# A second Strassen level for one more product of the last down projection: M7 split in seven, M6 ahead of it, operand sums of M7 and M4 on VectorE

## The chip, the cores and the metric

One core of one Trainium2 chip runs the whole kernel in one launch. The metric is the device time of one execution in microseconds (us), as the median of several runs. Engine names: PE is TensorE, DVE is VectorE, ACT is ScalarE, POOL is GpSimd, SP is SyncE, which here only issues DMAs.

## The reference

The input x has 2048 tokens of 1024 features, in bfloat16. The kernel is a layernorm, a linear-attention block and a gated feed-forward block, joined at the end:

```python
xn = _layernorm(x)
s = linear_attention(xn, wqkv, wo)            # 32 heads of 32
f = (silu(xn @ w_gate) * (xn @ w_up)) @ w_down  # 1024 -> 3584 -> 1024
out = x + s * silu(f)
```

What the change touches is the last matrix product, `h @ w_down`, with h of 2048 x 3584 and w_down of 3584 x 1024, for the second half of its tokens to be computed, and the two steps that follow it, silu and `x + s * g`.

## The kernel before

The feed-forward block runs in two passes of 1024 tokens. In each pass a loop of 28 steps (14 blocks of 256 columns of F, gate and up in turn) fills h, one 8-KB-per-partition weight tile a step; then comes the down projection. All products use Strassen's scheme in the form of Winograd: a product of 2x2 blocks is made from seven block products M1 to M7, whose operands are sums of blocks, and the results are added up afterwards.

The last pass's down projection is `emit_down_m`. h is seen as four blocks A11, A12, A21, A22, each of 512 tokens by 14 chunks of 128 of F. The sums S1 to S4 are made from them in place (S1 over A21, S2 over A11, S4 over A12), S3 in two tiles of its own (S3h). The weights of M1 to M7, sums of blocks of w_down, were made in the first pass and lie in DRAM. One product at the first level is 4 blocks of 128 tokens x 14 chunks = 56 matmuls of 512 columns; `prod_t(M, t, ...)` issues the 14 of one token block (L1439 in the profile).

M1, M2 and M4 (the tuple `L2`) go one level deeper: `l2_M` makes each from seven products again, each of 7 chunks x 2 token halves, with 256 columns (`l2_p`, L1475). Their operand sums are made by `l2_lhs`, four instructions for each of seven j, on POOL: for M2 all through the last pass into spare buffers (`x_spare`, "kept" in the profile), for M1 late in the pass into `r_spare`, for M4 during M7 into M2's buffers. `l2_M` moves part results between PSUM banks with copies on ACT (L1487, L1495) and adds to what is kept on DVE (L1427). It is a generator: it yields once after two products, and it calls `fill` between its sixth and its last product, so that another product's matmuls stand there on PE.

The second-level weights are prepared in the last pass's loop, in units of two j. `l2_load` (at the steps in `L2_UNITS`) has SP load four blocks into one of the two buffers in `r_spare`, which it takes in turn; `l2_sums`, one step later, makes four sums on POOL (L1149) and stores seven blocks to DRAM by a POOL DMA (L1150). The two buffers come out of the same eight as the weight tiles; from step `L2_FROM` on, POOL uses them for M1's operand sums. SP's queue is in program order: a load that waits for a buffer holds back the gate and up weights behind it.

The order on each engine is written by hand: it is the order of the program. In `emit_down_m` it is M1 and the first half of M2, M2 with M7's first token block as its fill, M7, M6, M5, M4 with M3's first token block as its fill, M3. KA holds M1 + ..., KB = KA + M7 + M6; `fin` multiplies by s and adds x (L1209, L1210) and has SP store the result, `flush` issues the waiting ones, and silu runs on ACT (L1461). `load(M, q)` lets SP go on to the weight tiles that follow in `w_seq`, in the order of `M_ORDER`, as buffers come free.

Of the kernel before, what the change touches and what calls it, by code (L numbers as in the profile page):

```python
# [10 lines left out]
ALU = mybir.AluOpType  # L11
# [10 lines left out]
def kernel(  # L22
# [11 lines left out]
    nc = tc.nc  # L34
# [13 lines left out]
    TPB = TB // P  # L48
# [4 lines left out]
    NFG = F // FW  # L53
# [133 lines left out]
    NPASS = NB // 2  # L187
    passes = list(range(NPASS - 1, -1, -1))
    NWA = NFG // 2
    M_ORDER = (1, 2, 7, 6, 5, 4, 3)  # L190
    L2 = (1, 2, 4)
    L2_ORDER = (1, 2, 5, 6, 7, 4, 3)
    L2_FROM = 20
    L2_UNITS = range(3, 18, 2)
    NQ = NFG // 2
    CH = CW // 2
    l2_drams = {}
# [756 lines left out]
    with ExitStack() as p3:  # L954
# [197 lines left out]
        def l2_bufs(M):  # L1152
            v = [x[:].rearrange("p a b -> p (a b)").bitcast(F16) for x in x_spare]
            if M == 1:
                v = [x[:].rearrange("p h a b -> p (h a b)").bitcast(F16) for x in r_spare]
            v = [x[:, 0:2 * NQ * 2 * P].rearrange("p (s j r n) -> p s j r n", s=2, j=NQ, r=2) for x in v]
            return [v[0][:, 0], v[0][:, 1], v[1][:, 0], v[1][:, 1]]

        def l2_quad(A, j):
            v = A[:, :, j].rearrange("p k (r t n) -> p k r t n", r=2, t=2)  # L1160
            return v[:, 0, :, 0], v[:, 1, :, 0], v[:, 0, :, 1], v[:, 1, :, 1]

        def l2_lhs(M, A, j, eng):
            a11, a12, a21, a22 = l2_quad(A, j)
            s1, s2, s3, s4 = [v[:, j] for v in l2_bufs(M)]
            eng.tensor_tensor(out=s1, in0=a21, in1=a22, op=ALU.add)
            eng.tensor_tensor(out=s2, in0=s1, in1=a11, op=ALU.subtract)
            eng.tensor_tensor(out=s3, in0=a11, in1=a21, op=ALU.subtract)
            eng.tensor_tensor(out=s4, in0=a12, in1=s2, op=ALU.subtract)

        def quads(h, a, t):
            return h[:].rearrange("p (j k a) t -> p k j a t", k=2, a=2)[:, :, :, a, t * TB:(t + 1) * TB]
# [230 lines left out]
        def emit_down_m(p, h, base):  # L1403
# [8 lines left out]
            def load(M, q=None):  # L1412

                n_ = max(i for i, key in enumerate(seq) if key[2][0] == M and q in (None, key[2][1])) + 1
                load_w_to(base + n_ + (NPK - 2 if M == 1 and q != 3 else NPK))

            def S3(k):
                return s3_[k // NWA][:, k % NWA]

            def lhs_of(M):  # L1420
                if M == 7:
                    return S3
                v = {1: A11, 2: A12, 3: S4, 4: A22, 5: S1, 6: S2}[M]
                return lambda k: v[:, k]

            def tt(out, a, b_, op=ALU.add):
                nc.vector.tensor_tensor(out=out, in0=a, in1=b_, op=op)  # L1427

            def sums(out, a, b_, op):
                for k in range(0, NFG, 2):  # L1430
                    tt(out[:, k:k + 2], a[:, k:k + 2], b_[:, k:k + 2], op)

            def w_of(M, k):
# [8 lines left out]
            def prod_t(M, t, out, first):  # L1442
                for k in range(NFG):
                    mm(M, t, k, out, first)
# [5 lines left out]
            def banks(n=TPB):  # L1450
                turn[0] += 1
                pool, tg = (pps, "s") if turn[0] % 2 else (ppm, "m")
                return [pool.tile([P, CW], FP32, name="dm", tag=tg)[:] for _ in range(n)]

            def kept(nm):
                v = [m4.tile([P, 2, CW], FP32, name=nm, tag="m4") for _ in range(TPB // 2)]
                return [v[t // 2][:, t % 2] for t in range(TPB)]

            def silu(c, nm):
                g_ = k2([P, CW], BF16, nm)[:]  # L1460
                nc.scalar.activation(out=g_, in_=c, func=ACT.Silu, scale=rch)  # L1461
                return g_
# [15 lines left out]
            def l2_M(M, A, K, done, fill, in_place, dst=None):  # L1478


                bk = banks()
                lo, hi = slice(0, CH), slice(CH, CW)
                xw, zy = bk[0::2], bk[1::2]
                for r in range(2):
                    l2_p(M, 1, r, A, bk)
                for r in range(2):
                    nc.scalar.copy(out=zy[r][:, hi], in_=xw[r][:, lo])  # L1487
                for r in range(2):
                    l2_p(M, 2, r, A, bk)
                load(M, 0)  # L1490
                yield
                for r in range(2):
                    l2_p(M, 5, r, A, bk)
                    l2_p(M, 6, r, A, bk)
                    nc.scalar.copy(out=zy[r][:, lo], in_=zy[r][:, hi])  # L1495
                load(M, 1)
                for r in range(2):
                    l2_p(M, 7, r, A, bk)
                if K is None:
                    c = [dst[0:2], dst[2:4]]  # L1500
                else:
                    c = [[k2([P, CW], FP32, "l2c")[:] for _ in range(2)] for r in range(2)]
                for r in range(2):
                    c0, c1 = c[r]
                    if K is None:
                        nc.scalar.copy(out=c1[:, hi], in_=zy[r][:, lo])
                        nc.scalar.copy(out=c0[:, hi], in_=zy[r][:, hi])
                        nc.scalar.copy(out=c0[:, lo], in_=xw[r][:, lo])
                    else:
                        tt(c1[:, hi], zy[r][:, lo], K[2 * r + 1][:, hi])  # L1510
                        tt(K[2 * r][:, hi] if in_place else c0[:, hi], zy[r][:, hi], K[2 * r][:, hi])
                        if not in_place:
                            tt(c0[:, lo], xw[r][:, lo], K[2 * r][:, lo])
                    tt(c1[:, hi], xw[r][:, hi], c1[:, hi])
                fill()
                for r in range(2):
                    l2_p(M, 4, r, A, bk)
                load(M, 2)
                for r in range(2):
                    c0, c1 = c[r]  # L1520
                    if K is None:
                        nc.scalar.copy(out=c1[:, lo], in_=zy[r][:, lo])
                    else:
                        tt(c1[:, lo], zy[r][:, lo], K[2 * r + 1][:, lo])
                        done(2 * r + 1, c1)
                    l2_p(M, 3, r, A, bk)
                    if in_place:
                        tt(c0, xw[r], K[2 * r])
                    else:
                        tt(c0[:, hi], xw[r][:, hi], c0[:, hi])  # L1530
                    if done is not None:
                        done(2 * r, c0)
                load(M, 3)

            def go(g):
                for _ in g:
                    pass

            fins = deque()

            def flush(n=99):
                while fins and n:
                    fin(p, *fins.popleft(), *EV)
                    n -= 1

            load_w_to(base + NPK - 2)
            KA = kept("kA")
            fins = deque()
            M7, M6, M5 = [], [], []
            KB = []  # L1550

            def fill7():
                M7.extend(banks())
                KB.extend(kept("kB"))
                prod_t(7, 0, M7[0], True)

            def done2(t, c):
                fins.append((t, 0, silu(c, "g11")))
            m2 = l2_M(2, quads(h, 1, 0), KA, done2, fill7, False)
            for k in range(NFG):  # L1560
                tt(S3(k), A11[:, k], A21[:, k], ALU.subtract)
            go(l2_M(1, quads(h, 0, 0), None, None, lambda: next(m2), False, KA))
            sums(S1, A21, A22, ALU.add)
            go(m2)
            sums(S2, S1, A11, ALU.subtract)
            for t in range(TPB):
                if t:
                    prod_t(7, t, M7[t], True)
                tt(KB[t], M7[t], KA[t])
                flush(1)  # L1570
            load(7)
            sums(S4, A12, S2, ALU.subtract)
            for j in range(NQ):
                l2_lhs(4, quads(h, 1, 1), j, nc.gpsimd)
            M6 = banks()
            for t in range(TPB):
                prod_t(6, t, M6[t], True)
                tt(KB[t], M6[t], KB[t])
                tt(KA[t], M6[t], KA[t])
            load(6)  # L1580
            M5 = banks()
            for t in range(TPB):
                prod_t(5, t, M5[t], True)
                c = k2([P, CW], FP32, "c22")[:]
                tt(c, M5[t], KB[t])
                fins.append((t + TPB, 1, silu(c, "g22")))
                if len(fins) > 1:
                    flush(1)
            tt(KA[-1], M5[-1], KA[-1])
            load(5)  # L1590
# [215 lines left out]
```

## Time and profile before

| | |
|---|---|
| median of 3 runs | 756.01 us (755.42 to 756.09) |
| the profiled execution | 756.19 us, of which the span from first to last instruction is 754.4 us |
| PE busy | 742.7 us, 98% of the span, at the full granted clock |
| DVE, ACT, POOL busy | 580.5, 381.1, 398.6 us |
| down projection of the last pass | from 668.7 us to the end |
| M5's last product to M4's first | 726.4 us |

A profile is one execution. Times in it are microseconds from the start of the span; "L1439" is a line of the kernel. A row of the timeline gives start, duration, engine, line, operation, output<-input and count, and in brackets the idle time before it and what ended that. Durations of single instructions overlap the next one's start, so rates are taken from start to start.

### The profile page before, as it was taken

To read this page: it belongs to the slowest core of one execution; us is meant where nothing else is said; L and a number is where in the kernel's file an instruction comes from. 1 tells how busy PE (TensorE), PEld (TensorE's weight loads), DVE (VectorE), ACT (ScalarE), POOL (GpSimd) and SP (SyncE) were. 2 spreads that over 40 slices of the span, in tenths; PEclk is the share of its full clock that TensorE was granted. 3 is DMA by queue.
4 is the path that set the end of the run, shared out by engine and by line. 5 is a ranking of instruction groups with operands and counts; after the bars stand their busy time and mean duration, and the time that the engine had idled before them with its cause. 6 is when DMAs were issued, how large, how long until landed. Compare 5 with 4: busy or idle time off the path is not lost.

```text
span 754.4 us, 11017 instructions
## 1 busy us (share of the span) xinstructions
PE 742.7 (98%) x3793; PEld 361.3 (48%) x3857; DVE 580.5 (77%) x1040; ACT 381.1 (51%) x545; POOL 398.6 (53%) x500
## 2 busy tenths in 40 slices
PE   8999999999999999999999999999999999999997
PEld 3544444444454444444444444444444444467464
DVE  6687787887697788888889785458776767687966
ACT  5677766879966666656658311132323232232023
POOL 2444799998540266868685021811664555334900
PEclk9999999999999999999999999999999999999999
DMA  9967799869678668778799328789988774479652
GB/s 319 295 152 142 230 327 295 313 152 277 198 191 287 228 221 300 287 294 307 270 317 395 142 60 294 232 303 354 323 301 284 262 265 168 147 256 316 212 161 77
DMA packets 129160, 187.77 MB, mean 249 GB/s; under 512 B 36208, under 2 KB 104176, under 8 KB 119376
## 3 DMA queue, kind: packets, MB, share of 16 engines
q1 hardware_dynamic: 121760, 156.00, 64.3%
q0 software_dynamic: 5904, 28.58, 9.8%
q10 hardware_dynamic: 1440, 2.49, 0.9%
q8 instruction: 30, 0.49, 0.3%
q14 instruction: 26, 0.21, 0.1%
HBM read 119.47 MB, written 60.23 MB: 238 GB/s over the span
## 4 chain that ended last, share of the span: by engine, by line
PE 90%; DMA 3%; DVE 2%; POOL 1%; issue 1%; ACT 1%; SPq 0%; DVEq 0%; ACTq 0%; POOLq 0%
PE zw L968 25%; PE kv_ps L556 15%; PE xb L968 13%; PE q_ps L183 6%; PE yb L968 6%; PE dm L1439 6%; PE dm L1475 4%; PE dzw L1237 3%; PE fx L818 3%; PE s_ps L776 2%; PE dy L1237 2%; PE dx L1237 1%; DMA w_sb<-pk_g 1%; POOL w_sb L1137 1%; DMA w_sb<-pk_u 1%
## 5 line engine op out<-in xcount | busy, mean ns | idle before, releaser
L968 PEld LDWEIGHTS <-w_sb 128*128 128x128 f16 (+1 forms) x1568 | 152.1, 98 | 183.3 <-DMA w_sb<-pk_u 0.8
L968 PE MATMUL xb<-xnT,w_sb 128*128 128x512 bf16 x420 | 113.3, 379 | 1.5
L556 PE MATMUL kv_ps<-wkv_sb,xnT 128*128 128x512 bf16 x499 | 112.9, 379 | 1.3 <-ACT xnT L545 0.5
L968 PE MATMUL zw<-S,w_sb 128*128 128x512 f16 x448 | 105.8, 379 | 0.0
L968 PE MATMUL zw<-xnT,w_sb 128*128 128x512 bf16 x448 | 105.8, 379 | 0.0
L323 POOL TENSOR_TENSOR w_sb<-w_sb 128x512 f16<-128x512 bf16 x42 | 50.7, 1208 | 95.5 <-DVE w_sb L311 51.3
L288 ACT ACTIVATE w_sb<-w_sb 128x2048 bf16<-128x2048 bf16 x42 | 79.9, 1902 | 4.6 <-DMA w_sb<-in_B_w_up_dram 3.5
L556 PEld LDWEIGHTS <-xnT 128*128 128x128 bf16 x512 | 48.3, 98 | 56.1 <-ACT xnT L545 0.9
L183 PE MATMUL q_ps<-xnT,wq_sb 128*128 128x512 bf16 x249 | 58.0, 379 | 0.8 <-DVE pqT L151 0.4
L1044 ACT ACTIVATE sg<-cg 128x1024 bf16<-128x1024 f32 x28 | 29.6, 1057 | 57.4 <-DVE cg L1037 57.4
L968 PE MATMUL yb<-S,w_sb 128*128 128x512 f16 x224 | 57.4, 379 | 0.4 <-DMA w_sb<-pk_u 0.3
L1037 DVE SCALAR_TENSOR_TENSOR cg<-zw,rc_all,s 128x1024 f32<-128x1024 f32 x28 | 35.9, 1283 | 25.5 <-PE zw L968 13.9
L996 DVE SCALAR_TENSOR_TENSOR s<-yb,rc_all,s 128x512 f32<-128x512 f32 x42 | 31.4, 749 | 28.3 <-ACT s L995 28.3
L324 POOL TENSOR_TENSOR w_sb<-w_sb 128x512 f16<-128x512 bf16 x42 | 50.7, 1208 | 3.3
L326 POOL TENSOR_TENSOR w_sb<-w_sb 128x512 f16<-128x512 bf16 x42 | 50.3, 1199 | 0.0
L325 POOL TENSOR_TENSOR w_sb<-w_sb 128x512 f16<-128x512 bf16 x42 | 49.9, 1187 | 0.0
L1149 POOL TENSOR_TENSOR w_sb<-w_sb 128x512 f16<-128x512 bf16 (+3 forms) x32 | 33.1, 1056 | 29.9 <-DMA w_sb<-wd 29.2
L1211 POOL DMA_DIRECT2D out_dram<-io x16 | 8.7, 546 | 73.5 <-DVE io L1210 72.9
L995 ACT ACTIVATE s<-xb,rcl 128x512 f32<-128x512 f32 x14 | 9.6, 688 | 65.8 <-PE xb L968 65.8
L1237 PE MATMUL dx<-w_sb,hT 128*128 128x512 bf16 x108 | 40.9, 379 | 0.2
L995 ACT ACTIVATE s<-xb,rc_all 128x512 f32<-128x512 f32 x42 | 28.4, 675 | 21.9 <-issue 12.9
L311 DVE TENSOR_SCALAR w_sb<-w_sb,cs_all 128x2048 bf16<-128x2048 bf16 x35 | 36.3, 1038 | 2.8
(213 smaller groups left out, 1350.1 us busy)
## 6 DMA issues: line engine op xcount, KB each, us to landing
w_sb<-pk_g SPq DMA_DIRECT2D x27, 1024.0 KB, 6.0
pk_g<-w_sb SPq DMA_DIRECT2D x14, 1024.0 KB, 5.0
w_sb<-pk_u SPq DMA_DIRECT2D x14, 1024.0 KB, 6.0
pk_u<-w_sb POOLq DMA_DIRECT2D x13, 1024.0 KB, 5.4
w_sb<-l SPq DMA_DIRECT2D x9, 896.0 KB, 4.5
w_sb<-in_B_w_gate_dram SPq DMA_DIRECT2D x14, 512.0 KB, 6.3
w_sb<-in_B_w_down_dram SPq DMA_DIRECT2D x28, 256.0 KB, 4.4
w_sb<-in_B_w_up_dram SPq DMA_DIRECT2D x14, 512.0 KB, 5.4
```

Source lines behind the costliest of these rows:

```text
L183: nc.tensor.matmul(q_ps[:], lhsT=wq_sb[:, dc, g * P:(g + 1) * P], rhs=xn_ap(dc, btok), start=(dc == 0), stop=(dc == DC - 1))
L288: nc.scalar.activation(out=junk, in_=raw_view(key, t), func=ACT.Square, accum_out=asum[:])
L311: nc.vector.tensor_scalar(out=w, in0=w, scalar1=cs_all[:, c:c + 1], scalar2=None, op0=ALU.mult)
L323: nc.gpsimd.tensor_tensor(out=T1, in0=b12, in1=b11, op=ALU.subtract)
L324: nc.gpsimd.tensor_tensor(out=T2, in0=b22, in1=T1, op=ALU.subtract)
L325: nc.gpsimd.tensor_tensor(out=T3, in0=b22, in1=b12, op=ALU.subtract)
L326: nc.gpsimd.tensor_tensor(out=T4, in0=b21, in1=T2, op=ALU.subtract)
L556: mm = nc.tensor.matmul(kv_ps[:], lhsT=xn_ap(dc, tok), rhs=wkv_sb[:, dc, c * CW:(c + 1) * CW], start=(dc == 0), stop=(dc == DC - 1))
L968: mm = nc.tensor.matmul(out, lhsT=lhs(k), rhs=rhs(k), start=(first and k == 0), stop=(k == HK - 1), skip_group_check=True)
L995: nc.scalar.activation(out=s1[:], in_=x_[:], func=ACT.Copy, scale=rc)
L1237: nc.tensor.matmul(out, lhsT=lhs, rhs=rhs, start=first, stop=lastk, skip_group_check=True)
L1439: nc.tensor.matmul(out, lhsT=lhs_of(M)(k)[:, t * P:(t + 1) * P], rhs=w_of(M, k)[:, cols], start=first and k == 0, stop=k == NFG - 1, skip_ ...
```

## The change

M7 joins the products at the second level, and M6 is computed ahead of it. M7's operand is S3, now laid out so that the second level can take its quarters. Its operand sums, and those of M4, are made by a new `l2_lhs_r` on DVE, four instructions for each token half, in the buffers that M2's sums had; POOL no longer makes M4's. S3 and S1 are formed two chunks at a time; three of S1's seven sums stand ahead of M1 and four behind M1's first adds; S2 stands ahead of M2's adds, since M6 is M2's fill. KB is now written by M7's `l2_M`. M7's first token block is no longer a fill, and M5's first token block is M7's. The second-level weights of M7 are four more units of `l2_load` and `l2_sums`, twelve in place of eight, at two of every three steps in place of one of two.

```diff
-    M_ORDER = (1, 2, 7, 6, 5, 4, 3)
-    L2 = (1, 2, 4)
+    M_ORDER = (1, 2, 6, 7, 5, 4, 3)
+    L2 = (1, 2, 4, 7)
-    L2_FROM = 20
-    L2_UNITS = range(3, 18, 2)
+    L2_FROM = 22
+    L2_UNITS = (3, 4, 6, 7, 9, 10, 12, 13, 15, 16, 18, 19)
...
+        def l2_lhs_r(M, A, r, eng):
+            if not isinstance(A, tuple):
+                A = (A[:, 0], A[:, 1])
+            v = [a.rearrange("p j (r t n) -> p j r t n", r=2, t=2)[:, :, r] for a in A]
+            a11, a12, a21, a22 = v[0][:, :, 0], v[1][:, :, 0], v[0][:, :, 1], v[1][:, :, 1]
+            s1, s2, s3, s4 = [x[:, :, r] for x in l2_bufs(M)]
+            eng.tensor_tensor(out=s1, in0=a21, in1=a22, op=ALU.add)
+            eng.tensor_tensor(out=s2, in0=s1, in1=a11, op=ALU.subtract)
+            eng.tensor_tensor(out=s3, in0=a11, in1=a21, op=ALU.subtract)
+            eng.tensor_tensor(out=s4, in0=a12, in1=s2, op=ALU.subtract)
...
-            m2 = l2_M(2, quads(h, 1, 0), KA, done2, fill7, False)
-            for k in range(NFG):
-                tt(S3(k), A11[:, k], A21[:, k], ALU.subtract)
-            go(l2_M(1, quads(h, 0, 0), None, None, lambda: next(m2), False, KA))
-            sums(S1, A21, A22, ALU.add)
-            go(m2)
-            sums(S2, S1, A11, ALU.subtract)
+            S3 = tuple(x[:] for x in s3_)
+            m2 = l2_M(2, quads(h, 1, 0), KA, done2, fill6, False)
+            A11k, A21k = [v.rearrange("p (j k) t -> p k j t", k=2) for v in (A11, A21)]
+            for j0, j1 in ((0, 2), (2, 4), (4, 6), (6, 7)):
+                for k in range(2):
+                    tt(S3[k][:, j0:j1], A11k[:, k, j0:j1], A21k[:, k, j0:j1], ALU.subtract)
+
+            def fill2():
+                next(m2)
+                sums(S1, A21, A22, ALU.add, 6)
+            sums(S1, A21, A22, ALU.add, 0, 6)
+            go(l2_M(1, quads(h, 0, 0), None, None, fill2, False, KA))
+            sums(S2, S1, A11, ALU.subtract)
+            go(m2)
             for t in range(TPB):
                 if t:
-                    prod_t(7, t, M7[t], True)
-                tt(KB[t], M7[t], KA[t])
-                flush(1)
-            load(7)
+                    prod_t(6, t, M6[t], True)
+                if t in (0, 1):
+                    l2_lhs_r(7, S3, t, nc.vector)
+                tt(KA[t], M6[t], KA[t])
+                if t > 1:
+                    flush(2)
+            load(6)
             sums(S4, A12, S2, ALU.subtract)
-            for j in range(NQ):
-                l2_lhs(4, quads(h, 1, 1), j, nc.gpsimd)
-            M6 = banks()
+            KB = kept("kB")
+            go(l2_M(7, S3, KA, None, fill5, False, KB))
             for t in range(TPB):
-                prod_t(6, t, M6[t], True)
-                tt(KB[t], M6[t], KB[t])
-                tt(KA[t], M6[t], KA[t])
-            load(6)
-            M5 = banks()
-            for t in range(TPB):
-                prod_t(5, t, M5[t], True)
+                if t:
+                    prod_t(5, t, M5[t], True)
                 c = k2([P, CW], FP32, "c22")[:]
                 tt(c, M5[t], KB[t])
+                if t in (0, 1):
+                    l2_lhs_r(4, quads(h, 1, 1), t, nc.vector)
                 fins.append((t + TPB, 1, silu(c, "g22")))
-                if len(fins) > 1:
+                if t > 1:
                     flush(1)
```

More of the change, by code (lines that the diff above doesn't have):

```diff
@@ L1159, in l2_quad @@
         def l2_quad(A, j):
+            if isinstance(A, tuple):
+                v = [a[:, j].rearrange("p (r t n) -> p r t n", r=2, t=2) for a in A]
+                return v[0][:, :, 0], v[1][:, :, 0], v[0][:, :, 1], v[1][:, :, 1]
             v = A[:, :, j].rearrange("p k (r t n) -> p k r t n", r=2, t=2)
             return v[:, 0, :, 0], v[:, 1, :, 0], v[:, 0, :, 1], v[:, 1, :, 1]
+        def l2_lhs_r(M, A, r, eng):
[8 more added lines that the diff above has]
+            eng.tensor_tensor(out=s4, in0=a12, in1=s2, op=ALU.subtract)
         def l2_lhs(M, A, j, eng):
@@ L1415, in load @@
                 load_w_to(base + n_ + (NPK - 2 if M == 1 and q != 3 else NPK))
-            def S3(k):
-                return s3_[k // NWA][:, k % NWA]
             def lhs_of(M):
-                if M == 7:
-                    return S3
                 v = {1: A11, 2: A12, 3: S4, 4: A22, 5: S1, 6: S2}[M]
@@ L1427, in tt, with sums @@
                 nc.vector.tensor_tensor(out=out, in0=a, in1=b_, op=op)
-            def sums(out, a, b_, op):
-                for k in range(0, NFG, 2):
+            def sums(out, a, b_, op, k0=0, k1=NFG):
+                for k in range(k0, k1, 2):
                     tt(out[:, k:k + 2], a[:, k:k + 2], b_[:, k:k + 2], op)
@@ L1498, in l2_M @@
                     l2_p(M, 7, r, A, bk)
-                if K is None:
+                if dst is not None:
                     c = [dst[0:2], dst[2:4]]
@@ L1524, in l2_M @@
                         tt(c1[:, lo], zy[r][:, lo], K[2 * r + 1][:, lo])
+                    if done is not None:
                         done(2 * r + 1, c1)
@@ L1547, in emit_down_m, with fill6, fill5 @@
             KA = kept("kA")
[L1548 to L1555, printed above, removed]
+            M6, M5 = [], []
+            def fill6():
+                M6.extend(banks())
+                prod_t(6, 0, M6[0], True)
+            def fill5():
+                M5.extend(banks())
+                prod_t(5, 0, M5[0], True)
             def done2(t, c):
```

## The prediction

> **What bounds the kernel now.** I read the page first (busy time by engine, the slices), then the chain of waits over the last 200 us, then the timelines of DVE, PE, ACT and SP in the last pass, and last the DMA view of its first part.
>
> From the page:
>
> ```profile
> PE 742.7 (98%) x3793; PEld 361.3 (48%) x3857; DVE 580.5 (77%) x1040; ACT 381.1 (51%) x545; POOL 398.6 (53%) x500
> ```
>
> From the chain that ended last (start us, us, what):
>
> ```profile
> 668.90 18.34 PE dm L1475 x168
> 687.24 3.02 PE dm L1439 x14
> 690.26 3.06 PE dm L1475 x28
> 693.32 33.25 PE dm L1439 x154
> 726.60 0.70 DVE c L1427
> 727.32 0.72 ACT g L1461
> 728.37 6.27 PE dm L1475 x56
> ```
>
> PE is the bound. From 503 to 743.8 it stops only once: at 728, for 0.44 us, where M4's second product waits for a copy on ACT that stands behind the last silu of c22. Everything else (sums, evictions, weights) is hidden, so PE work that is removed here shortens the run unless a hidden part comes to light. After 743.8 the chain is DVE's multiplies and adds and the stores, 10.6 us, which the change leaves in the same order.
>
> **The PE term.** M7 before is 56 products of 512 columns (L1439). The chain gives 3.02 us for the first 14; the other 42 stand between 693.16 and 702.22 in PE's timeline, 9.06 us. Together 12.08, or 0.2157 each. The second level costs 7 products x 7 k-steps x 2 halves = 98 of 256 columns. The nearest row is M1 with M2, 18.34 us for 168, so 0.1092 each and 10.70 us for 98. The difference is **-1.38 us**. Both rates come from PE running without gaps; operand types (f16 against bf16) make no difference between the rows of L1475. M6, M5, M4 and M3 keep their counts.
>
> **What must stay hidden, in order of time.**
>
> *DVE around M1.* DVE's timeline, by window:
>
> ```profile
> 671.21 4.12 DVE L1427 TENSOR_TENSOR S3h<-hT 128x512 f16<-128x512 bf16 x5
> ...
> 683.03 1.89 DVE L1427 TENSOR_TENSOR hT<-hT 128x1024 f16<-128x1024 bf16 x3
> ...
> 696.73 4.38 DVE L1427 TENSOR_TENSOR hT<-hT 128x1024 f16<-128x1024 f16 x4
> ```
>
> The first and third rows run beside POOL sums, the second alone. Start to start, a 512-element sum takes 0.81 us beside POOL and 0.336 alone, one of 1024 takes 1.075 and 0.600. S3 is now six sums of 1024 and two of 512, then three sums of S1. POOL still has its last operand sums there (to 675 before, with the longer DVE sums to about 676.3), so I take five sums at 1.075: 676.58, then 0.60 and two of 0.336: 677.85, then S1's three: 679.65. M1's two adds into KA then end at 680.06 and 680.40. They must be done before M1's product 3 writes the same banks, at 680.97 and 681.74. Slack 0.9 us; cost taken as 0, upper bound under the rivals.
>
> *S1, S2 and M6.* S1's other four end at 682.8, M1's last two adds (PE is ready at 681.93 and 682.70) at 683.5, S2's seven sums, now without POOL beside them, at 687.7. M6 starts where M7 did, at 687.08, with k pair 0, whose S2 is ready at 684.1; the last pair is wanted at 689.7. M6's weights take the queue place that M7's had, with the same eight loads. Cost 0. M2's first adds start at 687.7, before they did at 688.67.
>
> *M7's operand sums on DVE.* Eight instructions of 7x128 = 896 elements, which no row shows; between 512 and 1024 alone that is 0.53 us, and the upper bound is 1.075, the contended row. POOL does nothing after 676 now, so I take 0.53 and 0.1 for a dependent start: about 2.2 us for four. With M2's adds done at 693.7, the four M6 adds (0.6 each) and the four multiply-add pairs of g11 (0.795 a pair alone, from 744.46 to 745.25), the sums end at 698.9, S4 at 708.8. M7 starts on PE at 702.22 and wants the sums at 705.3, its KB adds start at 709.3, and product 4 needs the first of them by 712.9. Slack 6 and 3 us. ACT is free when M7's four copies come, so they hide as they do for M1 and M2 (no gap on PE from 668.7 to 693). Cost 0.
>
> *M4's operand sums.* They go from POOL (which issued 28 and ended at 715.5) to DVE, behind the adds of c22 in M5: PE ends M5 at 725.0, DVE's sums end at 722.3, and c22's third add and a pair at 723.7, so the last c22 add is on time at 725.2. Wanted at 728.5: hidden. The stop at 728 stays, since the silu ahead of the copies still follows M5's last product; if it went too, the run would gain up to 0.44 more (754.2, inside the range).
>
> *SP in the M stage.* M7's four loads of 896 or 448 KB take the place of eight of 256 or 128 KB; they wait for buffers that PE frees by 685.6. M5's are landed by about 700 and wanted at 709.9. M4's and M3's wait for M6's and M7's buffers (700.7 to 715.9) and are wanted at 725 and 733. The flush with two pairs ahead of M3's first product puts 0.8 us more on DVE at 734.6 to 736.2, where c12 is wanted at 736.3. Cost 0.
>
> *The stream ahead of it.* M7's second-level weights are four units more on SP and POOL (steps 3 to 19 of the last pass). The DMA view from 515 to 640 (KB each, median us to landing) and POOL's timeline:
>
> ```profile
> l<-w_sb POOLq DMA_DIRECT2D x6, 896.0 KB, 7.9
> w_sb<-wd SPq DMA_DIRECT2D x28, 128.0 KB, 5.7
> ```
>
> ```profile
> 596.84 4.61 POOL L1149 TENSOR_TENSOR w_sb<-w_sb 128x512 f16<-128x512 f16 x4 [6.98 <-DMA w_sb<-wd]
> ```
>
> One unit holds its buffer for 1.6 (its four loads are issued over about 2.1 us, the last after 1.6) + 5.7 + 4.6 + 0.3 + 7.9 = 20.1 us. Before, a buffer came round every four steps, 24.2 us; now every three, 18.1 us. So SP will stand at the load of each odd unit, with gate and up weights behind it. The first unit loads at 520.5, its buffer is free at about 540, and the unit at step 18 loads at 540 + 4 x 20.1 = 620.4; the weight behind it issues at 623. PE wants that one at 666.15 - 5 x 6.045 = 635.9, so with 6.0 us to land (the page) it may issue until 629.9. Seven us are left; cost 0.
> The Trainium skill's page "DMA: Bandwidth & Descriptors", section "Anatomy of one DMA", gives 2.0 us + bytes / 436e3 for a GpSimd-issued DMA; for 896 KB that is an estimate of 4.1 us. By it the buffer would be free after 16.3 us, inside 18.1, and SP would never stand; the trace's 7.9 decides, and SP's wait has to be expected.
>
> **Sum.** The profiled execution took 756.19 us with a span of 754.4, 0.18 over the median. 754.4 - 1.38 = 753.0 of span; on the median, 756.01 - 1.38 = **754.6 us**. The three runs lie between 755.42 and 756.09. A measurement here can tell about 0.2%, 1.5 us, from no change, and the saving is just under that: the sign is clearer than the class.
>
> **Rivals.**
>
> *DVE late (0.14, 755.1 to 757.4).* DVE gets about 8.5 us of operand sums that POOL had or that did not exist, in a stage where it was busy 51.5 of 57.7 us. At 0.80 us each, halfway, M7's still hide and M4's eight push c22's last add from 725.2 to 725.8, and ACT's copies with it: 755.2. At 1.075, S4 ends at 713.1, the KB adds end 0.7 after PE wants product 4, and c22's last add comes 2.1 late on top: 756.01 - 1.38 + 2.8 = 757.4. Against it: POOL's 31 us in that stage are mostly gone, and with them the slow rows.
> The other place is M1's product 3, with 0.9 of slack: if POOL's last sums reach into S1's three, the adds come up to 1.4 later and PE stops 0.5, giving 755.1.
> The Trainium skill's page "SBUF — State Buffer", section "SBUF: two separate sides", says that the loser of the shared VectorE/GpSimd port waits for the whole instruction. By that a contended 1024 sum would be 0.60 + 0.63 = 1.23 and not 1.075; the slack there would shrink to 0.1, still without a stop. The rows here overlap by about 0.15.
>
> *Weights late (0.13, slower).* SP's stand behind the odd units decides from a buffer cycle of 540 + 4T + 2.5 = 629.9, T = 21.85 us; above that PE stops for 4 us for each us of T, at yb or xb on a weight tile. T = 22.2 takes back the saving (756.0), T = 23 gives 756.01 - 1.38 + 4.6 = 759.2. For it: two units in a row share the queue, and the DMA share was already 0.91 and 0.89 from 520 to 560. Against: at 20.1 the stream moves what it moved before in 12.1 us per unit, since SP's own wait thins it out.
>
> *The level does not pay (0.05).* If M7 stops as M4 did before its second product (0.44 with the missed start), 755.1.
>
> **How the numbers follow.** All hidden: 0.68, centred on 754.6 with the spread of the runs, 754.0 to 755.0; since the three runs reach 0.6 below their median and 0.1 above it, I put a little over half of it, 0.38, past the 1.5 us. Within 0.2%: the other 0.30 of it, most of DVE late (0.11), the level that does not pay (0.05) and the mildest of weights late (0.01), 0.47. Slower 0.15. The range reaches from the lowest run less the saving, 754.0, into the weights case at T = 22.35: 756.6.
>
> **What would show it.** M7 on the second-level line with 98 products in about 10.7 us and no PE wait between 668.7 and 725; M4 starting at 725.0 and not 726.4; no POOL sums after 677; SP waiting on stores of l at the odd units, but PE with no wait on w_sb from 515 to 666. The prediction is wrong if PE waits for DVE at L1475's counterpart in M1, M7 or M4, or for a pk tile.

## The result, and the profile after

| | before | after |
|---|---|---|
| median of 22 runs each | 755.49 us (754.91 to 756.67) | 754.39 us (753.34 to 755.96) |
| ratio after to before | | 0.9985, 95% interval 0.9979 to 0.9992 |
| the profiled execution, its span | 756.19, 754.4 us | 754.34, 752.6 us |
| M1's first product to M4's first, on PE | 57.65 us | 56.27 us |

The change saves 1.1 us, by the interval 0.6 to 1.6. The last line of the table comes from four rows of PE's timeline, two before and two after:

```profile
668.74 3.22 PE L1475 MATMUL dm<-w_sb,hT 128*128 128x256 bf16 x28
726.39 1.69 PE L1475 MATMUL dm<-w_sb,hT 128*128 128x256 f16 x14
```

```profile
667.93 3.22 PE L1484 MATMUL dm<-w_sb,hT 128*128 128x256 bf16 x28
724.20 1.69 PE L1484 MATMUL dm<-w_sb,hT 128*128 128x256 f16 x14
```

The lines that the prediction named have moved: L1439 is now L1448 (`prod_t`), L1475 is L1484 (`l2_p`), L1427 is L1436 (sums and adds on DVE), L1461 is L1470 (silu), L1487 is L1496 (the copies on ACT). L1172 to L1175 are the four sums of the new `l2_lhs_r`.

From the page after:

```profile
PE 740.8 (98%) x3835; PEld 365.2 (49%) x3899; DVE 577.7 (77%) x1054; ACT 382.5 (51%) x549; POOL 394.8 (52%) x492
```

PE has 42 more matmuls and 1.9 us less work, 1.38 us of it between M1 and M4. From the chain of waits (start us, us, what):

```profile
668.10 18.34 PE dm L1484 x168
686.43 3.02 PE dm L1448 x14
689.46 3.06 PE dm L1484 x28
692.51 9.06 PE dm L1448 x42
701.58 7.64 PE dm L1484 x70
709.22 3.02 PE dm L1448 x14
712.24 3.06 PE dm L1484 x28
715.30 9.08 PE dm L1448 x42
724.40 0.70 DVE c L1436
725.12 0.72 ACT g L1470
725.85 0.28 ACT dm L1496
```

M6 is the 3.02 and the 9.06 around M2's last 28, M7 the 70 and the 28 with M5's first 14 between them: `fill` stands behind five of the seven products (70 matmuls) and ahead of the last two, 4 and 3, and not behind the sixth as the description of the kernel above has it. M7 takes 7.64 + 3.06 = 10.70 us. PE has no gap from 668 to 724; the only wait of PE from 500 to 745 is still the one at M4's second product (the kernel before had one more, of 0.3 us for an up weight, that ended at 502.97):

```profile
PE dm L1484 <- ACT dm L1496: 0.3, 1, 0.3
```

DVE's timeline, with the rows on which the slack hung (start, duration of the group, engine, line, output<-input, count, and in brackets idle time before):

```profile
670.40 6.73 DVE L1436 TENSOR_TENSOR S3h<-hT 128x1024 f16<-128x1024 bf16 x8
677.05 1.88 DVE L1436 TENSOR_TENSOR hT<-hT 128x1024 f16<-128x1024 bf16 x3
678.86 0.74 DVE L1436 TENSOR_TENSOR kA<-dm,kA 128x256 f32<-128x256 f32 x2
...
697.55 0.62 DVE L1175 TENSOR_TENSOR kept<-S3h,kept 128x896 f16<-128x896 f16 x1
...
703.81 4.29 DVE L1436 TENSOR_TENSOR hT<-hT 128x1024 f16<-128x1024 bf16 x7
708.56 1.09 DVE L1436 TENSOR_TENSOR kB<-dm,kA 128x256 f32<-128x256 f32 x3 [0.46 <-PE dm L1484]
...
720.87 0.62 DVE L1175 TENSOR_TENSOR kept<-hT,kept 128x896 f16<-128x896 bf16 x1
...
724.40 0.69 DVE L1436 TENSOR_TENSOR c<-dm,kB 128x512 f32<-128x512 f32 x1 [1.53 <-PE dm L1448]
```

M1's first add into KA is done at 679.27 (678.86 + 0.41), 0.9 us before product 3 (680.16), M7's sums at 698.1, S4 at 708.0; ahead of the KB adds and of the last c22 add DVE waits for PE and not PE for DVE.

The stream from 515 to 650: SP's own waits (us in total, times, longest), then the DMA view (KB each, median us to landing):

```profile
SPq L1116 <- DMA l<-w_sb: 30.9, 10, 6.7
```

```profile
l<-w_sb POOLq DMA_DIRECT2D x9, 896.0 KB, 7.1
w_sb<-wd SPq DMA_DIRECT2D x42, 128.0 KB, 4.5
```

SP stands 31 us at the loads of the units, and PE waits for no weight.

### The profile page after: what moved, and what is told of

Same layout as the page of the kernel before. It is cut to its first block, busy times and chain, and to the rows that moved or that the text cites. A ratio compares the mean times of both kernels' runs of the same rounds, so it can differ in the third digit from the quotient of the medians.

```text
span 752.6 us, 11139 instructions
## 1 busy us (share of the span) xinstructions
PE 740.8 (98%) x3835; PEld 365.2 (49%) x3899; DVE 577.7 (77%) x1054; ACT 382.5 (51%) x549; POOL 394.8 (52%) x492
## 4 chain that ended last, share of the span: by engine, by line
PE 95%; DVE 2%; ACT 1%; issue 1%; DMA 0%; DVEq 0%; ACTq 0%
PE zw L968 26%; PE kv_ps L556 15%; PE xb L968 13%; PE yb L968 6%; PE q_ps L183 6%; PE dzw L1251 6%; PE dm L1484 6%; PE dm L1448 4%; PE dx L1251 3%; PE fx L818 3%; PE s_ps L776 2%; PE dy L1251 2%; PE kvz L578 1%; PE nd L745 1%; DVE w_sb L311 1%
## 5 line engine op out<-in xcount | busy, mean ns | idle before, releaser
L1149 POOL TENSOR_TENSOR w_sb<-w_sb 128x512 f16<-128x512 f16 (+3 forms) x48 | 50.3, 1069 | 18.0 <-DMA w_sb<-wd 17.3
```

The source lines that it names most:

```text
L1149: nc.gpsimd.tensor_tensor(out=b(o_), in0=b(a_), in1=b(b_), op=ALU.subtract)
```

## The experiments

The theory is that of the prediction: the saving is PE's, 98 matmuls of 256 columns for 56 of 512, and all the rest is hidden with little to spare. The rivals are that order and sums bring (or cost) something of their own, and that the stream does. The first two and the last two of these kernels were run five to eleven times each. The others were run once and are read by their traces.

**The stream alone.** The kernel before, with M7's four units added to the stream and not used.

```diff
-    L2_FROM = 20
-    L2_UNITS = range(3, 18, 2)
+    L2_FROM = 22
+    L2_UNITS = (3, 4, 6, 7, 9, 10, 12, 13, 15, 16, 18, 19)
-        l2_q = deque((M, j) for M in L2 if M != 2 for j in range(0, NQ, 2))
+        l2_q = deque((M, j) for M in (1, 4, 7) for j in range(0, NQ, 2))
```

> The kernel before with M7's second-level weights prepared as well (twelve units at the new steps, L2_FROM 22), and M7 still computed at the first level from its old weights: the stream alone, its result unused. Theory 'PE term': the stream is hidden, the time is that of before within 0.1% (755.5 +- 0.7); SP waits about 31 us for stores of l, as in the changed kernel (30.9 us, 10 times), and PE waits for no w_sb tile between 515 and 666 us. Rival 'weights late': 1 us or more slower than before, with PE waits on a pk tile.

Measured: 755.91 us against 755.58, ratio 1.0002 (0.9993 to 1.0011); 57.65 us from M1's start to M4's. SP's wait was 52.5 us in seven stands, more than the 31 of the changed kernel, and still no weight came late. The stream costs nothing in this stage, and at most 0.8 us in all by the interval.

**The order and the sums alone.** The changed kernel with M7 at the first level again.

```diff
-    L2 = (1, 2, 4, 7)
+    L2 = (1, 2, 4)
...
-            go(l2_M(7, S3, KA, None, fill5, False, KB))
+            M7 = banks()
+            for t in range(TPB):
+                prod_t(7, t, M7[t], True)
+                tt(KB[t], M7[t], KA[t])
+            load(7)
+            fill5()
```

> The changed kernel with M7 alone back at the first level (56 products of 512 columns, eight units of weights at the old steps); M6 ahead of M7, the sums of M4 on DVE and the order of S1, S2 and S3 stay. Theory 'PE term': the saving goes, the time is that of before within 0.1%, M4 starts 57.6 to 57.7 us after M1 on PE (before 726.39 - 668.74 = 57.65; changed 724.20 - 667.93 = 56.27). Rival 'the reordering pays': the time stays at the changed kernel's, 0.15% under before, because the gain came from the sums on DVE or the order and not from the products.

Measured: 755.86 us against 755.58, ratio 1.0003 (0.9994 to 1.0012); 57.66 us from M1 to M4. Without the second level the whole saving is gone. M6 ahead, S1 in two parts and M4's sums on DVE are worth nothing by themselves in this stage, and nothing that the interval could tell in the whole.

**M7's sums twice.** One line doubled: 4.5 us more on DVE ahead of S4.

```diff
                     l2_lhs_r(7, S3, t, nc.vector)
+                    l2_lhs_r(7, S3, t, nc.vector)
```

> The changed kernel with M7's eight operand sums on DVE made twice over (8 x 0.534 + 0.2 = 4.5 us more on DVE; same results). It tells how much DVE slack the change left. Theory: S4 then ends at 708.1 + 4.5 = 712.6 on the changed kernel's clock; the first KB add of M7 ends at 713.0 where PE's product 4 wants it by 712.1, the fifth at 714.3 where the second half wants it by 713.8 after the first stop: PE stops about 1.5 us in M7, M4 starts 57.8 us after M1 (56.27 + 1.5). Rival 'DVE has no slack': the whole 4.5 us comes through (60.8). Rival 'DVE is far off the path': no change (56.3).

Measured: 755.23 us; 57.37 us from M1 to M4, 1.10 more than the changed kernel, in two stops (1.5 was expected). PE's timeline:

```profile
712.38 0.93 PE L1484 MATMUL dm<-w_sb,S3h 128*128 128x256 f16 x7 [0.37 <-DVE kB L1436]
713.70 0.92 PE L1484 MATMUL dm<-w_sb,S3h 128*128 128x256 f16 x7 [0.40 <-DVE kB L1436]
```

So 3.4 of the 4.5 us were hidden: the slack ahead of the KB adds is there, and PE is next when it is used up. Product 4 starts at 712.38, just as the second KB add ends (711.91 + 0.42), not the first.

**All of S1 ahead of M1's adds.**

```diff
-                sums(S1, A21, A22, ALU.add, 6)
-            sums(S1, A21, A22, ALU.add, 0, 6)
+            sums(S1, A21, A22, ALU.add)
```

> The changed kernel with all seven of S1's sums ahead of M1's first two adds into KA, not three. Theory: those adds start 4 x 0.60 = 2.4 us later, the first ends at 681.7 on the changed kernel's clock where PE's product 3 of M1 wants it at 680.16: PE stops 1.5 us there, M4 starts about 57.8 us after M1, and the run is about 1.5 us longer. Rival 'M1 does not wait for that add': no change, 56.3.

Measured: 756.21 us; 57.83 us from M1 to M4. PE's timeline, and DVE's:

```profile
682.00 1.69 PE L1484 MATMUL dm<-w_sb 128*128 128x256 bf16 x14 [1.41 <-DMA w_sb<-wd]
```

```profile
681.53 0.74 DVE L1436 TENSOR_TENSOR kA<-dm,kA 128x256 f32<-128x256 f32 x2
```

The profile names a DMA for the stop, but the product starts at 682.00 just as the first KA add ends (681.53 + 0.41), and the stop is there only when four sums of S1 stand ahead of that add. Four sums moved are worth 1.6 us, more than the whole change brings.

**All operand sums on POOL.** Both calls of `l2_lhs_r`, M7's and M4's, on the other engine.

```diff
-                    l2_lhs_r(7, S3, t, nc.vector)
+                    l2_lhs_r(7, S3, t, nc.gpsimd)
-                    l2_lhs_r(4, quads(h, 1, 1), t, nc.vector)
+                    l2_lhs_r(4, quads(h, 1, 1), t, nc.gpsimd)
```

> The changed kernel with M7's and M4's operand sums (two times four instructions of 896 elements each) issued on POOL and not on DVE; all else is as changed. Theory (the saving is PE's 56 products of 512 columns against 98 of 256, and the place of the sums does not matter as long as they are ahead of their products): POOL took 1.155 us for a 512-element sum before (4.62 for four), so about 2.0 us for 896 and about 8 us for a row of four; M7's second row then ends near 710, and its products want the second row only from about 708, so PE stops by 2 us at the most, likelier 0 to 1; M4's second row ends near 731 and is wanted at about 730, a stop of 0 to 1.5. From M1's start to M4's on PE 56.3 to 57.3 us, total 754.5 to 756. Rival (the sums are only hidden because they are on DVE, and beside POOL DVE's own work goes at the contended 1.075 us instead of 0.600): DVE's evictions come late, PE waits for DVE on M7's product 4 and M4's first products, and M1's start to M4's is over 58.5 us, total over 757.

Measured: 759.04 us; 60.96 us from M1 to M4. My theory was wrong here and the rival right. POOL's sums were in time (M7's done at 701.9, and PE stopped for none), but DVE was not. DVE's timeline, one instruction a row in the first three:

```profile
700.19 1.98 DVE L1224 TENSOR_TENSOR io<-g,io 128x512 bf16<-128x512 bf16 x1
702.10 0.41 DVE L1223 TENSOR_TENSOR g<-g,io 128x512 bf16<-128x512 bf16 x1
702.55 0.42 DVE L1224 TENSOR_TENSOR io<-g,io 128x512 bf16<-128x512 bf16 x1
...
705.08 9.35 DVE L1436 TENSOR_TENSOR hT<-hT 128x1024 f16<-128x1024 bf16 x7
714.35 1.07 DVE L1436 TENSOR_TENSOR kB<-dm,kA 128x256 f32<-128x256 f32 x3
```

An add of 0.42 us takes 1.98 beside one POOL sum, and S4's seven sums take 9.35 us instead of 4.29: three of them start 2.29 us apart beside M4's sums on POOL, the others 0.60. Every one waits for nearly a whole POOL instruction (1.84 from start to start, alone). The KB adds come 6 us later, and PE stops 2.93 us at M7's product 4. That leaves 1.8 of the 4.7 us that were lost between M1 and M4, and the clock has them. Windows of this run (us, then PE, PE load, DVE, ACT, POOL busy with counts, granted PE clock, DMA share, GB/s):

```profile
709.00:712.00 3.00, 3.00 (x16) 1.40 (x15) 3.00 (x2) 0.00 (x0) 3.00 (x2) 1.00 0.91 313
715.15:718.30 3.15, 3.15 (x15) 2.22 (x15) 2.26 (x7) 0.00 (x0) 0.00 (x0) 0.50 0.80 309
718.30:720.00 1.70, 1.70 (x15) 1.43 (x14) 0.76 (x2) 0.00 (x0) 0.65 (x1) 0.95 0.29 59
```

After the stop the granted clock is 0.50 for the 3.2 us of the second window, and 15 matmuls take twice their time.

**M7's sums alone on POOL.**

```diff
-                    l2_lhs_r(7, S3, t, nc.vector)
+                    l2_lhs_r(7, S3, t, nc.gpsimd)
```

> The changed kernel with M7's operand sums alone on POOL; M4's stay on DVE. With both on POOL the run was 759.04 us, and PE stopped 2.9 us for the KB adds, which stood behind S4's sums on DVE, three of them 2.29 us apart beside POOL's sums for M4. Theory (it was M4's sums that met S4; M7's, done by 701.9 on POOL, are early enough): S4's seven sums take 4.3 us again, PE does not stop before M4, M1's start to M4's is 56.3 us, total 754 to 755. Rival (M7's own sums on POOL cost DVE the time, since they too slow the adds and pairs of M6, which then push S4): S4 ends over 1.5 us later than the 708.0 of the changed kernel, PE stops at M7's product 4, M1's start to M4's is 57.5 us or more, total over 755.5.

Measured: 755.03 us; 56.27 us from M1 to M4, no stop before M4, S4's seven sums in 4.30 us. The total is just above the expected 754 to 755; M1 started 0.7 us later than in the changed kernel. So it was M4's sums beside S4. M7's may stand on either engine as far as PE goes, though the KB adds come 0.75 us later after M1's start than with M7's sums on DVE; for M4's it matters.

**Five rows of M7's sums.** M7's sums on DVE twice, and the first row (the four sums of one token half) a third time: a stop as in the run with all sums on POOL, but without POOL.

```diff
                     l2_lhs_r(7, S3, t, nc.vector)
+                    l2_lhs_r(7, S3, t, nc.vector)
+                if t == 0:
+                    l2_lhs_r(7, S3, t, nc.vector)
```

> The changed kernel with M7's operand sums computed again on DVE: the first row three times, the second twice (twelve extra instructions, 6.6 us, all with the same result). With eight extra ones PE stopped for 0.54 and 0.56 us and its clock stayed at 1.00; after the 2.9 us stop of the run with all sums on POOL its clock was 0.50 for 3.2 us. Theory (the length of the stop sets the clock, whatever causes it): the extra row moves S4 and the KB adds 2.2 us further, the first stop becomes about 2.7 us, the granted clock falls to 0.50 for about 3 us behind it, and M1's start to M4's is 56.27 + 1.1 + 2.2 + 1.6 = 61.2 us, total about 759. Rival (the clock fell because of what POOL and the DMAs did in that run): the clock stays at 1.00, M1's start to M4's is about 59.6 us, total about 757.5.

Measured: 760.16 us; 61.28 us from M1 to M4. PE's timeline, then windows:

```profile
715.66 0.92 PE L1484 MATMUL dm<-w_sb,S3h 128*128 128x256 f16 x7 [2.63 <-DVE kB L1436]
716.99 1.23 PE L1484 MATMUL dm<-w_sb,S3h 128*128 128x256 f16 x7 [0.40 <-DVE kB L1436]
718.01 3.09 PE L1484 MATMUL dm<-w_sb,kept 128*128 128x256 f16 x14
```

```profile
715.66:716.40 0.74, 0.74 (x7) 0.66 (x7) 0.74 (x3) 0.00 (x0) 0.00 (x0) 1.00 0.91 289
717.00:717.80 0.80, 0.80 (x7) 0.63 (x6) 0.80 (x3) 0.00 (x0) 0.00 (x0) 0.79 0.85 255
718.00:719.00 1.00, 1.00 (x7) 0.74 (x5) 0.00 (x0) 0.00 (x0) 0.00 (x0) 0.50 0.14 30
```

The clock falls with POOL idle throughout, and stays at half where the DMAs are nearly idle too (0.14), so it is PE's stops that set it. It falls almost 2 us after PE has gone on. The 5.0 us that are lost are 3.0 of stops and 2.0 of half clock.

**A unit at every step.**

```diff
-    L2_UNITS = (3, 4, 6, 7, 9, 10, 12, 13, 15, 16, 18, 19)
+    L2_UNITS = range(3, 15)
```

> The changed kernel with its twelve second-level weight units one to a step, in steps 3 to 14, where they stood two to every three steps in steps 3 to 19. Nothing else is changed. Theory (the stream is hidden only as long as a unit's buffer comes round before the gate and up weights queued behind the next unit on SP are due): two buffers at 17.5 us a cycle give a unit every 8.75 us against one every 6.05 wanted, so the unit of step 13 loads at about 520.3 + 5 x 17.5 = 608 instead of 581, 27 us late, against about 18 us that the weights behind it have to spare; PE stops for a w_sb tile between about 590 and 640 by about 10 us in all (6 to 18, more if the cycle grows under the load), total 761 to 773. Rival (the weights are hidden anyway, because they are issued far ahead or the queue shares out): no PE wait on w_sb, total 754 to 755.

Measured: 768.94 us; M1 starts 14.6 us later than in the changed kernel, and that is the whole loss in span. PE's waits, and a window behind the first of them:

```profile
PE yb L968 <- DMA w_sb<-pk_u: 10.3, 3, 4.2
```

```profile
589.84:592.50 2.66, 2.66 (x7) 1.00 (x8) 0.00 (x0) 0.00 (x0) 2.37 (x3) 0.50 1.14 292
```

The mechanism of the rival "weights late" exists: SP stands for the buffer, and the up weights behind it are late by 10.3 us in all (forecast 10). The way there was not quite the forecast one: the unit of step 13 loaded at 602.0 and not at 608, and it was the one behind it, at 614.9, that came 28 us late for its step. About 4 us more are half clock behind three stops of 3.5, 2.5 and 4.2 us, which no forecast had.

**The last stop of PE.** M4's first two products and their copies on ACT are issued ahead of the last silu of c22 (`out3`, `done4` and `fill3` move up with them).

```diff
                 if t in (0, 1):
                     l2_lhs_r(4, quads(h, 1, 1), t, nc.vector)
+                if t == TPB - 1:
+                    m4p = l2_M(4, quads(h, 1, 1), KB, done4, fill3, True)
+                    next(m4p)
                 fins.append((t + TPB, 1, silu(c, "g22")))
...
-            go(l2_M(4, quads(h, 1, 1), KB, done4, fill3, True))
+            go(m4p)
```

> The changed kernel with M4's opening (its first two products and the copies of them on ACT) issued ahead of the last silu of c22. Nothing is left out or added. Theory (the one stop of PE that is left from 503 on, 0.4 us before M4's second product, is ACT's copy standing behind that silu, as the trace names it): the stop goes, the silu comes some 0.6 us later and is hidden, and the run is 0.4 us shorter than the changed kernel: about 754.0, a ratio to the kernel before of 0.998. Rival (the second product would wait for something else just as long, DVE's add of c22 or M4's sums): the stop stays with another name, ratio as that of the changed kernel, 0.9985.

Measured: 753.95 us against 755.43, ratio 0.9976 (0.9966 to 0.9985). PE has no gap any more from M1 to M3; the chain goes from M5 through M4's 70 products in one piece:

```profile
719.96 4.32 PE dm L1448 x20
724.28 7.64 PE dm L1484 x70
```

From M4's start to the end of the span it is 27.98 us, against 28.40. The intervals of this ratio and of the changed kernel's overlap; the trace shows where the 0.4 went.

**The last work of DVE.** On top of that, two multiply-add pairs of g21 move ahead of c12's second add (the one behind M3's second token block), and one of g12 behind them. `out3` gets a flag that leaves its matmuls out.

```diff
-            out3(1)
+            prod_t(3, 1, M5[1], False)
+            fins.append(fins.popleft())
+            flush(2)
+            out3(1, False)
```

> The kernel of the experiment before with the order of DVE's last work changed: the two multiply-add pairs of g21's first rows go ahead of the last add of c12, and one pair of g12 behind them. Nothing is left out or added. Theory (the end is set by DVE, which works without a gap from about 741.6 to 749.7 on the pairs of the last two outputs; of these about 1.6 us can be done before M3's last product ends, when DVE is waiting): DVE's last run starts with less to do, the last store goes out 0.8 to 1.5 us earlier, total about 753.1, ratio to the kernel before about 0.9965 to 0.9975. Rival (the silus of g21 are not there in time, or the end is set by the stores and not by DVE): DVE waits ahead of c12, total as the experiment before or up to 1 us longer.

Measured: 752.77 us against 755.43, ratio 0.9960 (0.9947 to 0.9972), the fastest version here. From M4's start to the end it is 26.83 us, 1.15 less than without it. DVE was full from 741.65 to the stores in the changed kernel; now PE is the end (start us, us, what):

```profile
740.74 6.34 PE dm L1448 x32
747.08 0.02 issue
747.10 0.59 ACT g L1644
```

## Why the prediction was right, and where it was off

- **The PE term.** -1.38 us was worked out; M1's start to M4's went from 57.65 to 56.27, which is 1.38. With M7 at the first level it is back at 57.66, and three other kernels with the second level and no stop ahead of M4 (the two with the end reordered and the one with M7's sums on POOL) have 56.27 again.
- **The median.** 754.6 was 756.01 - 1.38. More runs put the kernel before at 755.49, half a microsecond lower; on that base the sum gives 754.1, and 754.39 was measured. The saving by the ratio, 0.6 to 1.6 us, holds the 1.38, and is below what was called measurable, as the larger of the chances had it. That 754.6 and 754.39 lie so close is partly luck: the base was 0.5 us too high, and the saving of the medians was 0.3 us below the sum. In the profiled executions the span is 1.8 us shorter: 1.38 in the stage, 0.8 ahead of M1, where M1's start also differs by 0.75 us between the two last experiments, which are the same up to there, and -0.4 behind DVE's last add, in the last store.
- **DVE around M1.** The slack of 0.9 us came out as forecast, at times 0.8 earlier. With the four sums of S1 ahead of the adds and not behind them, PE stops for 1.4.
- **M7's and M4's sums.** 0.53 us each was taken where no row showed such a sum, 0.534 was measured. They ended at 698.1 and 721.4 (forecast 698.9 and 722.3), S4 at 708.0 (708.8); 0.8 us of each difference is M1's earlier start. The slack of 3 us ahead of product 4 was 2.7 by the run with sums twice: the KB adds came 3.25 us later after M1's start, and product 4 was 0.54 us late. The forecast took the first KB add as the one that product 4 needs, and by the times it is the second, 0.33 us on.
- **The stop at M4's second product** stayed, and its cause was named rightly: with the copies ahead of the silu it is gone, for the 0.4 us that were put on it.
- **The stream.** SP stood for the units, as expected, and PE did not; but SP stood at all ten units behind the first two, and not only at the odd ones. The size was off: one of the two buffers was loaded at 520.33 and, five turns later, at 608.01, SP standing ahead of each load but the first: 17.5 us a turn, not 20.1. Two terms of that sum were too long, the load (5.7, measured 4.5) and the store (7.9, measured 7.1), together 2.0 of the 2.6 us; why they are shorter here is not shown. The unit of step 18 loaded at 608, not 620, so the margin was some 19 us and not 7. The estimate of 4.1 us for the store after the Trainium skill's page "DMA: Bandwidth & Descriptors", section "Anatomy of one DMA", stays far below the measured 7.1. The conclusion drawn from it, that SP would not stand where a turn is shorter than the 18.1 us between its loads, fails as well: it stood at 17.5. Before, where SP waited for PE alone, the load of step 7 started at 539.9; at 6.045 us a step that puts step 3 at 515.7, or 514.9 with M1's earlier start. The first load went out at 520.33, some 5 us behind that pace, and a turn of 17.5 makes up only 0.6 of it, so SP was still behind at the last unit. This is worked out from the rows; no run tests it.
- **The rivals.** "Weights late" is a real mechanism, but the kernel was further from its point than the forecast put it. "DVE late" took 1.075 us as the upper bound of a contended sum. That was measured beside POOL sums of 0.63 us, the only ones that the changed kernel has there, and S3's time came out by it; it is no bound beside other work on POOL: beside sums of 1.84 it is 2.29. The price also counted stops alone: in two runs a stop of 2.6 or 2.9 us brought 1.8 to 2.0 us of half clock on top.

## What to carry to other kernels

Here the work taken off the engine that bounds the kernel was worth its own duration in its stage, 1.38 us, and 1.1 (0.6 to 1.6) in the median; it needed each hidden chain behind it to have its slack worked out, 0.9 us at the nearest place. Stops of 2.5 us and more cost that engine more than their length, and a sum moved to an idle engine may be paid for by the engine beside it. The larger gains lay in the order of small work near the end: two moves of a few instructions brought 1.6 us more by the trace (28.40 - 26.83), and the second level 1.38.

## What was not expected of the hardware

- **PE's clock after a stop.** Behind stops of 2.5 to 4.2 us (five of them, in three kernels) the granted clock was 0.50 for 3.41 us each time by the trace's clock record, and cost 1.3 to 2.0 us more; behind stops of 0.4 and 1.4 us it stayed at 1.00. It fell before PE went on in three of the five and almost 2 us after in another. The Trainium skill's page "TensorE: Matmul & The Clock Gate", section "Part 1: The HAM clock gate", tells of a half clock after an idle window of about 3.4 us, in windows that run free of the program. The length of the slow stretch and the late fall go with that, and so do the three falls of the run with a unit at every step (589.33, 606.40, 623.47), 17.07 us apart, which is five times 3.41. That stops of 2.5 and 2.6 us were enough does not, if the window must be idle throughout: in the 3.41 us ahead of the late fall, PE was busy for 1.40 us. In the 3.41 us around the stop of 1.41 us it was busy for 2.00, and the clock stayed. Where between these two the fall begins was not measured.
- **DVE beside POOL.** The price of a contended DVE sum is nearly the whole POOL instruction: 0.60 + 0.63 would be 1.23 and was 1.075, 0.60 + 1.84 would be 2.44 and was 2.29. Both lie 0.15 below. The Trainium skill's page "SBUF — State Buffer", section "SBUF: two separate sides", has the loser wait for the whole instruction; up to these 0.15 us the runs agree. The profile counts that wait as DVE's busy time. It is not always DVE that pays: in both runs with M7's sums on POOL the first of them took 5.93 us, beside S2's seven sums on DVE, which took 4.29 us as they do alone.
- **Who is named for a wait.** PE's stop of 1.41 us is put down to a DMA in the trace, and the DVE add that ends there is what moves it.
